# Half of the second block's weights split into seven operands during the first block and kept in DRAM

## The chip, the cores and the metric

The kernel runs on one core of one Trainium2 chip. The time is the device time of one execution in microseconds (us), as the median of several runs; lower is better. Every product is made in fp32r, with each operand split into a high part (a cast) and a low part (the rest), so that three matmuls stand for one.

## The reference

Three stages, one after another, on 8 batches of 576 tokens with 8 heads of 64 (512 columns). The second and third are cut here to their core:

```python
def _moe_ref(x, w_in, w_out):            # 512 -> 2048 -> 512
    h = x @ w_in
    g = np.where(h > 0.0, h, alpha * (np.exp(np.minimum(h, 0.0)) - 1.0))
    return (g @ w_out).astype(np.float32)

def _moe2_ref(x, w1, w2, w3, w_out):     # 512 -> 768 -> 512
    h = np.maximum(np.maximum(x @ w1, x @ w2), x @ w3)
    return (h @ w_out).astype(np.float32)
```

The first is an attention with landmarks: queries and keys averaged over groups of 18 tokens, three softmaxes, and six Newton steps for an inverse. The weights come as float64, so the kernel reads them as pairs of 32-bit words and makes float32 of them itself.

## The kernel before, in words

**First block** (attention and the first feed-forward). It runs batch by batch; a batch has 32 slots. In each slot `h_mm` makes a 128x288 piece of the hidden layer in 6 matmuls into a PSUM tile `ph` (two buffers), ACT makes two exponentials `eh` of it, DVE ends `eh`, `split` makes the two parts `gt` (cast on ACT, low part on POOL), and three slots later `x_mm` multiplies them by w_out in 12 matmuls. Attention of the next batch is laid into the slots by a table of slot numbers (`STEP_SLOTS`). The result goes to DRAM as `xs`. The order of PE and DVE in this block is the program's; `plan[t]` lists what else slot t issues.

**Weights of the second block.** `Narrowing` loads a piece of w1, w2, w3 (three pieces each, of 256 of the 768 columns) or of w_out2 (three pieces of 256 rows), makes float32 of it (`widen`, `narrow`) and stores it as `w2s` in DRAM. There are 12 pieces, two in each of batches 1 to 6.

**Second block.** 9 token blocks `nb` of 512 tokens, in each 3 pieces `p` of 256 hidden columns, in each the three weights `i`. One such product is `u_mm`: a 2x2 block product in Winograd's form with 7 products, 42 matmuls of 128x256. It needs seven token operands (`Operands`) and seven weight operands, each split in two. `quarters` combines the products (`s`, `v`, `u`, `t` on ACT, DVE and POOL), the maximum over `i` is taken on DVE, and `keep` makes three sums `s` of the four quarters `t` and stores all seven as `hs` in DRAM: already the operands of the output. The weight operands stay in SBUF for all token blocks. They are made by nine jobs `weights2(p, i)`: the raw piece is loaded from `w2s` (`raw2`), 4 differences `tt` on DVE, four or five casts `w` on ACT (L958), and low parts `w` (L960) on POOL and DVE in turn. The jobs begin in slot 2 of the last batch and go on, one step at each call of `background`, into the second block. Their places come free one by one: those of the first piece (`pools["w"]`) once attention is done, others where w_out of the first block was last read.

**Output.** For each token block two `o_mm` of 63 matmuls, `hs` against w_out2. `weights3` makes w_out2's seven operands (128x768, both parts) in the last token block: 4 differences, 7 casts (L1013), 7 low parts (L1015, on DVE and POOL in turn), into the seven tiles of the first piece's weights. `Middle` loads `hs` as seven `hf` and splits each into `ho` (cast L1092 on ACT; low part L1094 on DVE, the third operand's on POOL). The loads of the first three operands use the tag `s3` with three buffers, which `keep` uses too.

All transfers are issued by SP, in one order. Lines of the profile that the text speaks of: L101 and L103 `split`, L235 attention's products, L675 `h_mm`, L679, L680 and L685 `eh`, L707 `x_mm`, L791 `difference`, L824 and L826 the token operands, L861, L863 and L876 the sums of a product, L995 `u_mm`, L1104 `o_mm`.

Of the kernel before, what the change touches and what calls it, by code (L numbers as in the profile page):

```python
# [9 lines left out]
F32 = mybir.dt.float32  # L10
F32R = mybir.dt.float32r
# [8 lines left out]
def landmark_attention_mlp_maxout_kernel(  # L20
# [65 lines left out]
    NP = KF2 // 2  # L86
    w2s = tc.dram_tile([3 * NP + KF2 // 2, P, 1024], F32, name="w2s")
    hs = tc.dram_tile([NT // 512, P, NP, 7, 256], F32, name="hs")
# [671 lines left out]
    )  # L760

    class Narrowing:


        def __init__(self, it):
            self.it = it

        def load(self):
            t = att.tile([P, CH, DM], U32, tag="v", name="words2")
            self.words = t[:, :4].rearrange("p a (c w) -> p (a c) w", w=2)  # L770
            i, p = divmod(self.it, NP)
# [18 lines left out]
    def difference(out, a, b):  # L790
        nc.vector.tensor_tensor(out=out, in0=a, in1=b, op=ALU.subtract)  # L791

# [94 lines left out]
    N1 = 3 * len(OPS)  # L887

    def w_place(q):

# [31 lines left out]
    def raw2(n):  # L922
        p, i = divmod(n, 3)
        src = w2s[i * NP + p].rearrange("p (c f j) -> p c f j", c=KD, f=2)
# [8 lines left out]
    def weights2(p, i):  # L933

        n = 3 * p + i
        if n not in raws:
# [68 lines left out]

    def weights3():

        l = pools["l"]

        def put(nm, v, n):  # L1010
            t = l.tile([P, 2, NP, 256], F32R, tag=f"b{n}", name="wo2")
            hi, lo = wb[nm] = (t[:, 0], t[:, 1])
            nc.scalar.copy(hi, v)  # L1013
            eng = nc.gpsimd if n % 2 else nc.vector
            eng.tensor_tensor(out=lo, in0=v, in1=hi.bitcast(F32), op=ALU.subtract)  # L1015

        raw = [l.tile([P, NP, DM], F32, tag=tag, name="raw") for tag in ("xf", "b6")]
        for f in range(2):
            nc.sync.dma_start(
                out=raw[f],  # L1020
                in_=w2s[3 * NP :].rearrange("a p (f c) -> p f a c", f=2)[:, f],
            )
        s = l.tile([P, NP, 256], F32, tag="s3", name="s", bufs=3)
        b11, b12, b21, b22 = [t[:, :, e * 256 : (e + 1) * 256] for t in raw for e in range(2)]
        yield
        difference(s, b12, b11)
        put("T1", s, 0)
        yield
        difference(b12, b22, b12)
        put("T3", b12, 1)  # L1030
        yield
        put("B11", b11, 2)
        yield
        difference(s, b22, s)
        put("T2", s, 3)
        yield
        put("B21", b21, 4)
        yield
        put("B22", b22, 5)
        yield  # L1040
        difference(b11, b21, s)
        put("N4", b11, 6)
        yield


# [269 lines left out]
    for b in range(1, B):  # L1315
# [9 lines left out]
        for n in range(NCH):  # L1325
            at(t0 + NSL + (W_SLOTS if b > 1 else SECOND_W)[n], w_step, b, n, True)
    for it in range(3 * NP + KF2 // 2):
        nw = Narrowing(it)
        t0 = (1 + it // 2) * NSL + (15, 23)[it % 2]
        at(t0, nw.load)  # L1330
        run = nw.run()
        for n in range(4):
            at(t0 + 4 + n, next, run, None)
    manual = ExitStack()
    for t, sl in enumerate(seq):
# [8 lines left out]
        for fn in late:  # L1344
            if callable(fn):
                fn()
        if t >= LAG:
            x_mm(*seq[t - LAG])
        i = t - (B - 1) * NSL
        if i == 2:  # L1350
# [3 lines left out]
            tk = tokens(0)  # L1354
            jobs += [weights2(n // 3, n % 3) for n in range(9)]
        if i > KF and (i - KF) % FPN == FPN - 1:
            free += [f"wp{(i - KF) // FPN}{g}" for g in range(2)]
        if i > KF + LAG and (i - KF - LAG) % 2:
            passed.add((i - KF - LAG) // 2)
        if i > 2:  # L1360
# [8 lines left out]
    while tk.make():  # L1369
        pass  # L1370
    passed |= set(range(KF // 2))

    r_s.release()
# [6 lines left out]
        tc.tile_pool(name="ps_u", bufs=8, space=PSUM, reuse_waits="tile")  # L1380
    )


    for nb in range(NBL):
        nxt = tokens(nb + 1) if nb + 1 < NBL else None
        for p in range(NP):
# [27 lines left out]
    while len(ahead.raw) < len(OPS):  # L1414
        ahead.load()
    free += [(r_w, f"wo{m}") for m in range(5, KF // 2)]
# [59 lines left out]
```

## Time and profile before

| | before |
|---|---|
| time, median of 3 runs | 1374.45 us (1373.82 to 1375.12) |
| profiled execution | 1371.51 us |
| its span | 1369.7 us |
| PE busy | 1307.7 us (95%) |
| DVE busy | 842.6 us (62%) |
| ACT busy | 682.2 us (50%) |
| POOL busy | 678.8 us (50%) |
| DMA | 152.30 MB, 111 GB/s over the span |

The span is what the trace covers; the execution's time holds 1.8 us more. Busy time says which engine is full on average; the stages differ, so the prediction reads the trace stage by stage. The first block lasts until about 805 us, the second until 1225, the output until the end.

### The profile page before, as it was taken

Reading aid. Unit: us, or ns where it says so; the run is one execution under the profiler, and the core shown is the slowest. Engines: PE = TensorE matmul, PEld = TensorE weight load, DVE = VectorE, ACT = ScalarE, POOL = GpSimd, SP = SyncE. Lnnn points to the kernel's source line nnn. Section 1 sums busy time; section 2 is a strip of 40 time slices with the busy share of each in tenths; the row PEclk is TensorE's granted clock in tenths of the full one; section 3 lists DMA queues with packets and bytes.
Section 4 is the critical chain, followed back from the end, with each engine's and each line's share of the span. In section 5 each row is a group of like instructions: output and inputs, shape, how many; then the busy total and the mean of one; then the engine's idle time right before and its main releaser. Section 6 shows DMA issues by size and latency. Waiting matters only on the chain.

```text
span 1369.7 us, 28360 instructions
## 1 busy us (share of the span) xinstructions
PE 1307.7 (95%) x11144; PEld 1231.0 (90%) x11144; DVE 842.6 (62%) x1603; ACT 682.2 (50%) x1555; POOL 678.8 (50%) x671
## 2 busy tenths in 40 slices
PE   4588999999999999999999998999999999989998
PEld 2477899899998998998989998999999999989998
DVE  6885745436446455365453468776677667787673
ACT  4784556656656656566566643232133212345451
POOL 2781423424325334243355557666666666685543
PEclk8699999999999999999999999999999999999999
DMA  9635104204223042042132112221222122249882
GB/s 359 223 107 167 35 19 164 69 32 134 68 86 129 19 158 74 33 133 69 38 121 63 34 64 100 86 85 58 109 85 86 59 108 86 99 137 325 291 257 78
DMA packets 91590, 152.30 MB, mean 111 GB/s; under 512 B 5312, under 2 KB 49472, under 8 KB 91456
## 3 DMA queue, kind: packets, MB, share of 16 engines
q1 hardware_dynamic: 91456, 150.49, 32.0%
q8 instruction: 87, 1.43, 0.4%
q14 instruction: 47, 0.39, 0.1%
HBM read 99.35 MB, written 51.12 MB: 110 GB/s over the span
## 4 chain that ended last, share of the span: by engine, by line
PE 82%; DVE 6%; DMA 4%; ACT 3%; POOL 3%; issue 2%; SPq 0%; DVEq 0%; POOLq 0%; ACTq 0%
PE x L707 28%; PE p L995 24%; PE ph L675 14%; PE p L1104 10%; PE banks L235 6%; DMA words<-in_moe_w_out_dram 2%; DMA raw<-w2s 1%; POOL u L863 1%; DVE tt L791 1%; DMA kT<-in_k_dram 1%; ACT words L122 1%; DVE wf L128 0%; DMA hf<-hs 0%; ACT eh L679 0%; ACT gt L101 0%
## 5 line engine op out<-in xcount | busy, mean ns | idle before, releaser
L707 PE MATMUL x<-gt,wo 128*128 128x288 f32 x3072 | 468.0, 301 | 6.3 <-DVE gt L103 2.2
L707 PEld LDWEIGHTS x<-gt,wo 128*128 128x128 f32 x3072 | 422.0, 189 | 47.4 <-issue 22.3
L995 PE MATMUL p<-xo,w 128*128 128x256 f32 x3402 | 413.0, 284 | 7.2 <-ACT w L958 3.9
L995 PEld LDWEIGHTS p<-xo,w 128*128 128x128 f32 x3402 | 410.9, 191 | 9.4 <-ACT w L958 4.1
L103 POOL TENSOR_TENSOR gt<-eh,gt 128x288 fp32r<-128x288 f32 x243 | 198.0, 818 | 366.9 <-ACT gt L101 338.3
L675 PE MATMUL ph<-ah,wp 128*128 128x288 f32 x1024 | 249.6, 299 | 11.4 <-DVE eh L685 5.4
L685 DVE SCALAR_TENSOR_TENSOR eh<-eh,ph 128x288 f32<-128x288 f32 x256 | 114.2, 447 | 161.5 <-ACT eh L680 129.7
L863 POOL TENSOR_TENSOR u<-s,v 128x512 f32<-128x512 f32 x99 | 136.4, 1377 | 134.5 <-DVE v L861 134.5
L675 PEld LDWEIGHTS ph<-ah,wp 128*128 128x128 f32 x1024 | 180.3, 190 | 19.4 <-DVE eh L685 9.2
L679 ACT ACTIVATE eh<-ph 128x288 f32<-128x288 f32 x256 | 104.6, 410 | 125.8 <-PE ph L675 97.2
L101 ACT CAST gt<-eh 128x288 fp32r<-128x288 f32 x256 | 110.2, 431 | 112.0 <-DVE eh L685 111.6
L675 PE MATMUL ph<-al,wp 128*128 128x288 f32 x512 | 152.7, 298 | 2.1 <-POOL al L103 2.1
L852 ACT COPY s<-p 128x512 f32<-128x512 f32 x99 | 58.0, 586 | 173.5 <-PE p L995 135.1
L1104 PE MATMUL p<-wo,ho 128*128 128x256 f32 x1134 | 136.4, 283 | 3.8 <-ACT ho L1092 2.0
L1104 PEld LDWEIGHTS p<-wo,ho 128*128 128x128 f32 x1134 | 135.9, 191 | 4.2 <-ACT ho L1092 2.2
L680 ACT ACTIVATE eh<-eh 128x288 f32<-128x288 f32 x256 | 113.6, 445 | 5.3
L675 PEld LDWEIGHTS ph<-al,wp 128*128 128x128 f32 x512 | 97.3, 190 | 2.5 <-POOL al L103 2.5
L876 DVE TENSOR_TENSOR t<-p,u 128x512 f32<-128x512 f32 x81 | 55.7, 688 | 65.0 <-POOL u L863 62.7
L1002 DVE TENSOR_TENSOR t<-t 128x1024 f32<-128x1024 f32 x54 | 71.4, 1323 | 9.5 <-POOL t L866 3.8
L1094 DVE TENSOR_TENSOR ho<-hf,ho 128x768 fp32r<-128x768 f32 x54 | 65.4, 1237 | 17.4 <-ACT ho L1092 17.0
L1092 ACT CAST ho<-hf 128x768 fp32r<-128x768 f32 x63 | 51.3, 836 | 41.4 <-PE p L1104 22.5
L866 POOL TENSOR_TENSOR t<-u,s 128x256 f32<-128x256 f32 x81 | 67.7, 836 | 5.0
(167 smaller groups left out, 1387.5 us busy)
## 6 DMA issues: line engine op xcount, KB each, us to landing
hf<-hs SPq DMA_DIRECT2D x63, 384.0 KB, 5.6
hs<-t SPq DMA_DIRECT2D x27, 512.0 KB, 2.6
xs<-xo SPq DMA_DIRECT2D x36, 288.0 KB, 2.9
hs<-s SPq DMA_DIRECT2D x27, 384.0 KB, 2.9
qT<-in_q_dram SPq DMA_DIRECT2D x16, 576.0 KB, 6.3
kT<-in_k_dram SPq DMA_DIRECT2D x16, 576.0 KB, 7.4
words<-in_moe_w_dram SPq DMA_DIRECT2D x9, 1024.0 KB, 5.3
xf<-xs SPq DMA_DIRECT2D x9, 1024.0 KB, 5.0
```

Source lines behind the costliest of these rows:

```text
L101: nc.scalar.copy(hi, src)
L103: eng.tensor_tensor(out=lo, in0=src, in1=hi.bitcast(F32), op=ALU.subtract)
L235: ins = fn(*args, **kw)
L675: nc.tensor.matmul(ph[:, :HF], a, c, start=(g == 0 and j == 0), stop=(g == 1 and j == 2))
L679: nc.scalar.activation(e, ph[:, :HF], AF.Relu, scale=-1.0)
L680: nc.scalar.activation(e, e, AF.Exp, scale=-1.0)
L685: state["post"] = nc.vector.scalar_tensor_tensor(out=e, in0=e, scalar=1.0, in1=ph[:, :HF], op0=ALU.subtract, op1=ALU.max)
L707: nc.tensor.matmul(xacc[ec][:, :HF], a, gt[:, c], start=(first and j == 0), stop=(last and j == 2),)
L863: nc.gpsimd.tensor_tensor(out=u57, in0=s57, in1=v.unsqueeze(1).to_broadcast([P, 2, 256]), op=ALU.add)
L995: nc.tensor.matmul(dst, l, r, start=(c == 0 and j == 0), stop=(c == 1 and j == 2))
L1002: nc.vector.tensor_tensor(out=t, in0=t, in1=cur, op=ALU.max)
L1104: nc.tensor.matmul(dst, l, r, start=(c == 0 and n == 0), stop=(c == NP - 1 and n == 2))
```

## The change

Of the 12 pieces the three of w3 (`i == 2`) and the three of w_out2 are treated in a new way. `Narrowing` makes float32 of them as before, and in seven of the following slots (`behind`, slots 2 to 8 of the next batch) makes from them the seven operands in both parts, 4 differences `wt` on DVE, 7 casts `wq` on ACT, 7 low parts `wq` on POOL, and stores them as `wus` (w3) or `w3s` (w_out2). Their plain form isn't stored any more. In the second block `fetch_ready` loads w3's operands into the places where the jobs put them before (16 loads, 5.5 MB, where the raw pieces were 1.5 MB), and six jobs `weights2` are left. `fetch3` loads w_out2's operands, seven loads of 768 KB (5.5 MB, before 1.5 MB), after the first piece of the last token block; `weights3` is gone. All seven `hf` of the first output block are asked for after the second piece (before: five), with two more places for `ho`. The launch gets `dynamic_dma_scratch_size=1024`.

```diff
     class Narrowing:
-        def __init__(self, it):
-            self.it = it
+        def __init__(self, i, p):
+            self.i, self.p = i, p
...
-            for h, (_, f) in enumerate(halves):
-                nc.sync.dma_start(out=w2s[self.it][:, h * 512 : (h + 1) * 512], in_=f)
+            self.f = [f for _, f in halves]
+            if self.i < 2:
+                for h, f in enumerate(self.f):
+                    nc.sync.dma_start(
+                        out=w2s[self.i * NP + self.p][:, h * 512 : (h + 1) * 512], in_=f
+                    )
+
+        def put(self, nm, v):
+            k = [w for _, w in OPS].index(nm)
+            o = r_s.tile([P, 2, 256], F32R, tag="wq", name="wq", bufs=4)
+            hi, lo = [o[:, n] for n in range(2)]
...
+            split(v, hi, lo)
+            there = wus[:, self.p, k] if self.i < 3 else w3s[:, k, :, self.p]
+            nc.sync.dma_start(out=there, in_=o.bitcast(F32))
+
+        def parts(self):
...
+            t1, v1 = temp()
+            difference(v1, b12, b11)
+            self.put("B11", b11)
+            yield
+            t2, v2 = temp()
+            difference(v2, b22, v1)
+            self.put("T1", t1)
+            yield
...
+    def fetch_ready(q0, q1):
+        q = q0
+        while q < q1:
+            (u, k), (hi, lo, n) = divmod(q, 7), w_place(q)
+            n = min(n, q1 - q, 7 - k)
+            if u % 3 == 2:
+                for t, h in ((hi, 0), (lo, 1)):
+                    nc.sync.dma_start(out=t[:, :n].bitcast(F32), in_=wus[:, u // 3, k : k + n, h])
...
-    def weights3():
...
+    def fetch3():
+        for k in range(len(OPS)):
+            t = pools["l"].tile([P, 2, NP, 256], F32R, tag=f"b{k}", name="wo2")
+            nc.sync.dma_start(out=t.bitcast(F32), in_=w3s[:, k])
+            wb[OPS[k][1]] = [t[:, h] for h in range(2)]
...
-    for it in range(3 * NP + KF2 // 2):
-        nw = Narrowing(it)
-        t0 = (1 + it // 2) * NSL + (15, 23)[it % 2]
-        at(t0, nw.load)
-        run = nw.run()
-        for n in range(4):
-            at(t0 + 4 + n, next, run, None)
+    plain = [(i, p) for p in range(NP) for i in range(2)]
+    split7 = [(2, p) for p in range(NP)] + [(3, p) for p in range(NP)]
+    behind = [[] for _ in range(len(seq))]
+    for it in range(2 * NP):
+        for n, (nw, t0) in enumerate(((Narrowing(*plain[it]), 15), (Narrowing(*split7[it]), 23))):
+            t0 += (1 + it) * NSL
+            at(t0, nw.load)
+            run = nw.run()
+            for m in range(3):
+                at(t0 + 4 + m, next, run, None)
+            if n:
+                parts = nw.parts()
+                for m in range(7):
+                    behind[t0 + 11 + m].append(parts)
...
-            jobs += [weights2(n // 3, n % 3) for n in range(9)]
+            fetch_ready(0, N1)
+            jobs += [weights2(n // 2, n % 2) for n in range(2 * NP)]
...
+            fetch_ready(N1 + 4 * m, N1 + 4 * m + 4)
...
             if nxt is None and p == 0:
-                jobs.append(weights3())
+                fetch3()
...
-                for _ in range(5):
+                for _ in OPS:
                     ahead.load()
...
+                free += [(pools["r"], f"e{n}") for n in range(2)]
```

The order of PE's instructions is the same in both kernels. On the others instructions move, at three places above all. (Line numbers in the rows are those of each kernel; the changed one has them two higher in the first block; there `difference` is L765, the sums of a product are L916, L925 and L931, `raw` is loaded in L995, `xf` in L1037. A number behind a name tells tiles of that name apart.)

**ACT in the first slots of a middle batch.** `xo` ends a half of the batch before, `e` is attention's softmax. Before:

```order
L733 COPY xo<-x_2660 128x288
L101 CAST gt<-eh 128x288
L679 ACTIVATE eh<-ph 128x288
L680 ACTIVATE eh<-eh 128x288
L101 CAST gt<-eh 128x288
L679 ACTIVATE eh<-ph 128x288
L680 ACTIVATE eh<-eh 128x288
L337 COPY e<-banks 128x288 x2
L101 CAST gt<-eh 128x288
L679 ACTIVATE eh<-ph 128x288
L680 ACTIVATE eh<-eh 128x288
L337 COPY e<-banks 128x288 x2
```

With the change:

```order
L735 COPY xo<-x_2662 128x288
L103 CAST gt<-eh 128x288
L103 CAST wq<-wt 128x256
L103 CAST wq<-wf_2948 128x256 x2
L681 ACTIVATE eh<-ph 128x288
L682 ACTIVATE eh<-eh 128x288
L681 ACTIVATE eh<-ph 128x288
L103 CAST gt<-eh 128x288
L103 CAST wq<-wt 128x256
L682 ACTIVATE eh<-eh 128x288
L339 COPY e<-banks 128x288 x2
L103 CAST gt<-eh 128x288
```

Between the exponentials now stand the casts `wq`, three in one slot and one in each of those that follow.

**SP at the start of the last batch**, where the second block's first loads are issued (`xf` tokens, `raw` plain pieces). Before:

```order
L788 DMA w2s<-wf_8977 128x512
L788 DMA w2s<-wf_8980 128x512
L969 DMA xf<-xs 128x4x512
L927 DMA raw<-w2s 128x4x128
L927 DMA raw<-w2s 128x2x128 x2
L927 DMA raw<-w2s 128x4x128
L927 DMA raw<-w2s 128x2x128 x2
```

With the change:

```order
L809 DMA w3s<-wq 128x2x256
L1037 DMA xf<-xs 128x4x512
L952 DMA w_9431<-wus 128x4x256
L952 DMA w_9432<-wus 128x4x256
L952 DMA w_9433<-wus 128x3x256 x2
L995 DMA raw<-w2s 128x4x128
L995 DMA raw<-w2s 128x2x128 x2
L995 DMA raw<-w2s 128x4x128
L995 DMA raw<-w2s 128x2x128
```

Four loads of ready operands (`w<-wus`) stand ahead of the raw pieces.

**DVE in the last token block**, from the second piece's first product on (`v`, `t` sums of a product, L1002 or L1070 the maximum, `raw` w_out2). Before:

```order
L861 TENSOR_TENSOR v<-p_15118,s_15135 128x256
L870 TENSOR_TENSOR t<-p_15142,s_15135 128x256
L791 TENSOR_TENSOR raw<-raw 128x3x256
L1015 TENSOR_TENSOR wo_15198<-raw,wo_15198 128x768
L1015 TENSOR_TENSOR wo_15126<-s,wo_15126 128x768
L876 TENSOR_TENSOR t<-p_15154,u_15139 128x512
L791 TENSOR_TENSOR s<-raw,s 128x768
L861 TENSOR_TENSOR v<-p_15191,s_15207 128x256
L870 TENSOR_TENSOR t<-p_15214,s_15207 128x256
L791 TENSOR_TENSOR raw<-raw,s 128x3x256
L1015 TENSOR_TENSOR wo_15239<-raw,wo_15239 128x768
L876 TENSOR_TENSOR t<-p_15225,u_15211 128x512
```

With the change, the same products:

```order
L916 TENSOR_TENSOR v<-p_15294,s_15307 128x256
L925 TENSOR_TENSOR t<-p_15314,s_15307 128x256
L931 TENSOR_TENSOR t<-p_15322,u_15311 128x512
L916 TENSOR_TENSOR v<-p_15352,s_15365 128x256
L925 TENSOR_TENSOR t<-p_15372,s_15365 128x256
L931 TENSOR_TENSOR t<-p_15380,u_15369 128x512
L1070 TENSOR_TENSOR t<-t 128x1024
```

The differences and low parts of w_out2 are gone from between the products' sums.

## Rows read from the trace of the kernel before

**Rows 1.** The windows by stage: stretch, length, busy of each engine, granted clock, DMA share, GB/s.

```profile
205.00:297.20 92.20, 92.20 (x828) 84.39 (x827) 48.16 (x119) 55.87 (x139) 34.59 (x41) 1.00 0.26 87
805.10:880.20 75.10, 68.05 (x543) 67.43 (x544) 59.72 (x88) 24.85 (x52) 49.07 (x44) 0.95 0.26 88
880.20:1176.00 295.80, 295.80 (x2456) 294.64 (x2455) 201.53 (x304) 78.78 (x159) 189.01 (x176) 1.00 0.22 85
1225.00:1250.30 25.30, 21.46 (x158) 21.05 (x157) 17.46 (x23) 11.60 (x18) 15.30 (x12) 0.87 0.79 260
1250.30:1365.30 115.00, 114.96 (x980) 114.75 (x979) 74.04 (x89) 53.09 (x80) 52.98 (x40) 1.00 0.71 236
```

**Rows 2.** PE's waits between 805 and 881 us: releaser, total us, times, longest.

```profile
PE p L995 <- ACT w L958: 3.9, 1, 3.9
PE p L995 <- ACT xo L824: 1.7, 1, 1.7
PE p L995 <- POOL w L960: 1.5, 1, 1.5
```

**Rows 3.** The window after PE's first long wait in the output.

```profile
1232.00:1236.00 4.00, 3.45 (x16) 3.45 (x17) 2.78 (x4) 0.83 (x1) 1.46 (x3) 0.50 0.07 17
```

**Rows 4.** PE's waits between 1200 and 1260 us.

```profile
PE p L1104 <- ACT ho L1092: 2.0, 1, 2.0
PE p L1104 <- POOL ho L1094: 1.8, 1, 1.8
```

**Rows 5.** PE's timeline at the start of the output: start, duration, and idle before.

```profile
1224.99 2.27 PE L1104 MATMUL p<-wo,ho 128*128 128x256 f32 x18
1229.30 1.44 PE L1104 MATMUL p<-wo,ho 128*128 128x256 f32 x10 [2.03 <-ACT ho L1092]
```

**Rows 6.** SP's timeline, the loads of `hf` behind the last stores.

```profile
1224.74 11.57 SPq L1079 DMA_DIRECT2D hf<-hs  x6
```

**Rows 7.** ACT's timeline, the third operand's high part.

```profile
1228.41 0.83 ACT L1092 CAST ho<-hf 128x768 fp32r<-128x768 f32 x1 [2.54 <-DMA hf<-hs]
```

**Rows 8.** POOL's timeline: an `u` of the last piece, and the third operand's low part.

```profile
1220.18 1.30 POOL L863 TENSOR_TENSOR u<-s,v 128x512 f32<-128x512 f32 x1 [3.29 <-DVE v L861]
1230.68 1.81 POOL L1094 TENSOR_TENSOR ho<-hf,ho 128x768 fp32r<-128x768 f32 x1
```

**Rows 9.** DVE's timeline in the last token block.

```profile
1202.96 2.61 DVE L1015 TENSOR_TENSOR wo<-s,wo 128x768 fp32r<-128x768 f32 x1
1222.74 0.95 DVE L1094 TENSOR_TENSOR ho<-hf,ho 128x768 fp32r<-128x768 f32 x1
```

**Rows 10.** The window in which w_out2's operands are made.

```profile
1200.00:1212.00 12.00, 12.00 (x102) 12.00 (x101) 11.05 (x11) 5.55 (x10) 12.00 (x7) 1.00 0.19 76
```

**Rows 11.** Groups by line and form, 700 to 880 us: count, busy, mean ns, idle before.

```profile
L958 ACT CAST w<-raw 128x256 fp32r<-128x256 f32 x9 | 3.6, 404 | 3.0 <-DMA raw<-w2s 2.1 <-PE x L707 0.9
L960 POOL TENSOR_TENSOR w<-raw,w 128x256 fp32r<-128x256 f32 x9 | 8.5, 946 | 0.0
L791 DVE TENSOR_TENSOR tt<-raw 128x256 f32<-128x256 f32 x18 | 11.4, 651 | 2.1 <-DMA raw<-w2s 2.1
```

**Rows 12.** DVE's timeline in the handover: one operation at two durations.

```profile
840.37 1.40 DVE L791 TENSOR_TENSOR tt<-raw,tt 128x256 f32<-128x256 f32 x1
850.15 0.41 DVE L791 TENSOR_TENSOR tt<-raw,tt 128x256 f32<-128x256 f32 x1
```

**Rows 13.** DVE's timeline in a middle batch.

```profile
464.24 0.45 DVE L685 SCALAR_TENSOR_TENSOR eh<-eh,ph 128x288 f32<-128x288 f32 x1 [2.19 <-ACT eh L680]
```

**Rows 14.** PE's timeline there: the next slot's first product.

```profile
465.58 0.29 PE L675 MATMUL ph<-ah,wp 128*128 128x288 f32 x1
```

**Rows 15.** PE's timeline: the last read of `w_in_sb`.

```profile
723.74 1.09 PE L235 MATMUL banks<-w_in_sb,mt 64*32 64x512 f32 x16
```

**Rows 16.** ACT's timeline: the first cast of a weight piece.

```profile
730.25 0.61 ACT L958 CAST w<-raw 128x512 fp32r<-128x512 f32 x1
```

**Rows 17.** The page's DMA issues: count, KB each, us to landing.

```profile
hf<-hs SPq DMA_DIRECT2D x63, 384.0 KB, 5.6
```

More of the change, by code (lines that the diff above doesn't have):

```diff
@@ L86, in landmark_attention_mlp_maxout_kernel @@
     NP = KF2 // 2
-    w2s = tc.dram_tile([3 * NP + KF2 // 2, P, 1024], F32, name="w2s")
+    w2s = tc.dram_tile([2 * NP, P, 1024], F32, name="w2s")
+    wus = tc.dram_tile([P, NP, 7, 2, 256], F32, name="wus")
+    w3s = tc.dram_tile([P, 7, 2, NP, 256], F32, name="w3s")
     hs = tc.dram_tile([NT // 512, P, NP, 7, 256], F32, name="hs")
@@ L760, in landmark_attention_mlp_maxout_kernel, with difference @@
     )
+    def difference(out, a, b):
+        nc.vector.tensor_tensor(out=out, in0=a, in1=b, op=ALU.subtract)
     class Narrowing:
-        def __init__(self, it):
-            self.it = it
+        def __init__(self, i, p):
+            self.i, self.p = i, p
         def load(self):
@@ L786, in run, with temp @@
                 yield
-            for h, (_, f) in enumerate(halves):
-                nc.sync.dma_start(out=w2s[self.it][:, h * 512 : (h + 1) * 512], in_=f)
-    def difference(out, a, b):
-        nc.vector.tensor_tensor(out=out, in0=a, in1=b, op=ALU.subtract)
+            self.f = [f for _, f in halves]
[8 more added lines that the diff above has]
+            hi, lo = [o[:, n] for n in range(2)]
+            if self.i < 3 and nm[0] == "B":
+                hi, lo = [t.rearrange("p (c j) -> p c j", c=2) for t in (hi, lo)]
+            split(v, hi, lo)
+            there = wus[:, self.p, k] if self.i < 3 else w3s[:, k, :, self.p]
+            nc.sync.dma_start(out=there, in_=o.bitcast(F32))
+        def parts(self):
+            if self.i < 3:
+                b11, b12, b21, b22 = [
+                    f.rearrange("p (c h j) -> p c h j", c=2, h=2)[:, :, e]
+                    for f in self.f
+                    for e in range(2)
+                ]
+            else:
+                b11, b12, b21, b22 = [f[:, e * 256 : (e + 1) * 256] for f in self.f for e in range(2)]
+            def temp():
+                t = r_s.tile([P, 256], F32, tag="wt", name="wt", bufs=4)
+                return t, (t.rearrange("p (c j) -> p c j", c=2) if self.i < 3 else t)
+            t1, v1 = temp()
[6 more added lines that the diff above has]
+            yield
+            t3, v3 = temp()
+            difference(v3, b22, b12)
+            self.put("B22", b22)
+            yield
+            t4, v4 = temp()
+            difference(v4, b21, v2)
+            self.put("B21", b21)
+            yield
+            self.put("T2", t2)
+            yield
+            self.put("T3", t3)
+            yield
+            self.put("N4", t4)
+            yield
     class Operands:
@@ L887, in landmark_attention_mlp_maxout_kernel @@
     N1 = 3 * len(OPS)
+    def fetch_ready(q0, q1):
[6 more added lines that the diff above has]
+                    nc.sync.dma_start(out=t[:, :n].bitcast(F32), in_=wus[:, u // 3, k : k + n, h])
+                for m in range(n):
+                    wb[u // 3, 2, OPS[k + m][1]] = (hi[:, m], lo[:, m])
+            q += n
     def w_place(q):
@@ L922, in raw2 @@
     def raw2(n):
-        p, i = divmod(n, 3)
+        p, i = divmod(n, 2)
         src = w2s[i * NP + p].rearrange("p (c f j) -> p c f j", c=KD, f=2)
@@ L933, in weights2 @@
     def weights2(p, i):
-        n = 3 * p + i
+        n = 2 * p + i
         if n not in raws:
@@ L1003, in u_mm @@
         return t
-    def weights3():
[L1008 to L1043, printed above, removed]
+    def fetch3():
[3 more added lines that the diff above has]
+            wb[OPS[k][1]] = [t[:, h] for h in range(2)]
     KEPT = (4, 1, 0, 5, 2, 6, 3)
@@ L1346, in landmark_attention_mlp_maxout_kernel @@
                 fn()
+        for parts in behind[t]:
+            next(parts, None)
         if t >= LAG:
@@ L1358, in landmark_attention_mlp_maxout_kernel @@
         if i > KF + LAG and (i - KF - LAG) % 2:
-            passed.add((i - KF - LAG) // 2)
+            m = (i - KF - LAG) // 2
+            passed.add(m)
+            fetch_ready(N1 + 4 * m, N1 + 4 * m + 4)
         if i > 2:
@@ L1371, in landmark_attention_mlp_maxout_kernel @@
     passed |= set(range(KF // 2))
+    fetch_ready(N1 + 2 * KF - 8, N1 + 2 * KF)
     r_s.release()
@@ L1381, in landmark_attention_mlp_maxout_kernel @@
     )
+    fetch_ready(N1 + 2 * KF, 3 * N1)
     for nb in range(NBL):
@@ L1408, in landmark_attention_mlp_maxout_kernel @@
                 ahead = Middle(0)
-                for _ in range(5):
+                for _ in OPS:
                     ahead.load()
                 free = [(r_w, f"wo{m}") for m in range(5)]
+                free += [(pools["r"], f"e{n}") for n in range(2)]
         tk = nxt
-    while len(ahead.raw) < len(OPS):
-        ahead.load()
     free += [(r_w, f"wo{m}") for m in range(5, KF // 2)]
```

4 lines of the change are left out of this document (2 added, 2 removed).

## The prediction, made before the changed kernel ran

> **What bounds the kernel now.** I read the windows by stage first, then what PE waits for in the two stages where it isn't full, then the timelines around those waits. The windows show that TensorE sets the time nearly everywhere: in a middle batch of the first block it is busy for 92.20 of 92.20 us, in the steady part of the second block for 295.80 of 295.80, in the output for 114.96 of 115.00, at a granted clock of 1.00 [rows 1]. What can be won lies in the two rows that are left, the handover into the second block (805.1 to 880.2 us, clock 0.95) and the start of the output (1225.0 to 1250.3, clock 0.87) [rows 1].
>
> Their loss is worked out against the steady stage of the same products. Second block: 295.80/2456 = 0.1204 us a matmul [rows 1]; the handover has 543 of them, 65.4 us at that pace, and takes 75.1. **9.7 us are lost**; 3.9 + 1.7 + 1.5 = 7.1 us of that are PE waiting, for a weight's high part from ACT, an `xo` and a weight's low part from POOL [rows 2], and the remaining 2.6 lie in the clock. Output: 114.96/980 = 0.1173 us [rows 1]; 158 of them are 18.5 us, and the stretch takes 25.3. **6.8 us are lost**; 2.0 + 1.8 = 3.8 us are PE waiting for `ho`, ACT's and then POOL's [rows 4], and the other 3.0 again the clock: after these waits the granted clock is 0.50, the lower of the two levels (1.2 GHz) [rows 3]. So ending the waits should give their clock back as well.
>
> Why they occur. In the handover DVE is busy for 59.72 of 75.10 us [rows 1] with the token operands, the sums of the products and the last four weight jobs; the 3.9 us wait is for an ACT cast which itself waits for DVE's differences. In the last token block making w_out2's operands fills DVE for 11.05 and POOL for 12.00 of 12 us [rows 10], a single low part taking 2.61 [rows 9]. The backlog is still there in the last piece: POOL waits 3.29 us for DVE's `v` [rows 8]. The store of `keep` is late by it, and behind that store SP issues the load of the third operand at 1224.74 [rows 6]; ACT casts it at 1228.41 [rows 7], POOL makes its low part from 1230.68, in 1.81 us [rows 8]. PE had come to it at 1224.99 + 2.27 = 1227.3 [rows 5].
>
> **The change, part by part.**
>
> *Second block, weights of w3.* Three of the nine `weights2` jobs go; of the four that DVE still had to do in the handover, one is left. What takes their place are loads only, and the handover moves no more than 88 GB/s at a DMA share of 0.26 [rows 1], so they have room; the loads for the second and third piece are let go by the last matmuls of the first block and are wanted some 25 and 40 us later (five and eight products of 42 × 0.1204 = 5.06 us, [rows 1]). I take the whole 9.7 us as gone, and put 0.5 back for what isn't the weights' fault: the 1.7 us for `xo` [rows 2] need not vanish, so bounds 0 to 1.7, nearer to 0 because that operand was late behind the same DVE queue.
>
> *Last token block, w_out2.* Seven casts, seven low parts and four differences become seven loads of 768 KB. 5.5 MB at the 260 GB/s of the output's start [rows 1] are 21 us, over the 30 us that the second and third pieces take before the output (six products); all seven are issued ahead of the third operand's load, and none waits for an engine that is behind. With the backlog gone, the third operand's load is set by the buffer that it takes over: it must wait until DVE has made the low part of the first operand. The last piece's first group ends on PE two products before the output, 1224.99 − 2 × 5.06 = 1214.9 [rows 1, 5]; its `v`, `u` (1.30, [rows 8]), `t` and two `ho` of 0.95 [rows 9] put the load at about 1219 instead of 1224.74. It lands 5.6 us later (median of such loads, [rows 17]), at 1224.6; cast 0.83, low part 1.81 [rows 7, 8]: 1225.4 and 1227.3. PE wants the high part at 1227.3 and the low part some ten matmuls later, at 1228.5 [rows 5]. That is in time by 1 to 2 us, so the whole 6.8 us is taken as gone, with a margin thin enough to be a rival.
>
> *First block, batches 2 to 7.* Each gets seven parts: 7 ACT casts of 128x256 (0.40 us, [rows 11]: 2.8 us a batch), 4 DVE differences (0.65: 2.6 us), 7 POOL low parts (0.95: 6.6 us) and 7 stores of 256 KB on SP, two stores of the plain piece less for half of them. The engines have the time: 55.87, 48.16 and 34.59 us are used of 92.20 [rows 1]. The stores add at most 1.8 MB in 92.2 us, 19 GB/s to 87 [rows 1]. What can hurt is the place: the casts stand in slots 2 to 8, where ACT also does the exponentials of attention, and `eh` on DVE sets when PE may reuse `ph`'s two buffers. The tightest place that I found has DVE ending `eh` at 464.24 + 0.45 = 464.69 [rows 13], and PE starting the product that needs it at 465.58 [rows 14]: 0.9 us of slack, and there ACT would now carry a cast or two (0.4 to 0.8). Elsewhere it is wider. Cost: nothing in most batches, a few tenths in some; 0.5 us over six batches. Bounds 0 and 7 (every batch loses three casts, 1.2 us). SP's loads of q, k, v and words stand behind the new stores, which wait for POOL's low parts; those loads are issued half a batch ahead, and this cover hides it.
>
> *Start of the last batch.* Loads of 512, 512, 384 and 384 KB now stand on SP ahead of the raw pieces, and the first must wait until PE has read `w_in_sb` for the last time, 723.74 + 1.09 = 724.8 [rows 15]. 1.8 MB at 260 GB/s [rows 1] take 6.9 us: 731.7; the first raw piece (512 KB, 2.0 us) is there at about 734, while ACT cast from it at 730.25 [rows 16]. ACT waits some 3.5 us with `eh` casts queued behind; `ph`'s second buffer covers at most a slot, 92.2/32 = 2.9 us [rows 1]. I put 1.0 us; bounds 0 (the transfers run at full rate, or the cast is reached later) and 5 (the whole wait).
>
> **Sum.** The profiled execution took 1371.5 us (span 1369.7 and 1.8 around it). 1371.5 − 9.7 + 0.5 − 6.8 + 0.5 + 1.0 = 1357.0. That execution lies 2.9 us below the median of the three timed runs, 1374.45; the forecast for the median is **1360 us**. A difference of less than 0.2% (2.7 us) can't be told from none.
>
> **A rule against it.** One DVE difference of two SBUF operands, 128x256, takes 0.41 us when undisturbed and 1.40 us in the same stretch beside POOL [rows 12]; so POOL's work delays DVE. The Trainium skill, "SBUF — State Buffer", section "SBUF: two separate sides", says that such a DVE operation and a GpSimd one share a port pair as an exclusive lock: who comes second waits for the whole instruction. The rows agree in direction (1.0 us added is about one POOL instruction). The first block gets 7 POOL instructions and 4 such differences a batch; if each difference met one and `eh` stood behind it, that is rival 2.
>
> **The rivals.**
>
> 1. *Only the handover pays.* The third operand is late again: its load stands behind seven transfers of 768 KB and SP's other stores, and a landing 2 us later eats the margin. As one late operand also costs the clock, take the whole 6.8 back: 1367. For it: 1 to 2 us of margin against landing times up to 5.6 us [rows 17]. Against: the load itself is released 5 us sooner. Chance 0.14.
> 2. *Slower: the first block pays.* In slots 2 to 8 of batches 2 to 7 the seven casts (0.40 each) and four differences held up by a POOL instruction (0.95 each, [rows 11]) all stand ahead of an `eh`. 2.8 + 3.8 − 0.9 of slack = 5.7 us a batch, 34 in six: 1394. It decides from (16.5 − 1.5 + 2.7)/6 = 3.0 us a batch on, that is if over half of this is unhidden. Against it: ACT is free for 39% and DVE for 48% of the stage [rows 1], and `ph` has two buffers. Chance 0.06.
> 3. *The waits change their name.* 8 MB more are loaded through the same queue, and in this program each transfer waits for the one eight places before it; if the loads of w3's pieces or w_out2 come as late as their making did, the gain is given back: 1374. Against it: room for 25 us and more, DMA share 0.26 [rows 1]. Chance 0.05.
>
> **How the numbers follow.** The forecast has 0.75, the rivals 0.14, 0.06 and 0.05. The forecast's own bounds: −1.5 (no price anywhere) to +8 (7 and 5 aren't met together) give 1358.5 to 1368, and 3 us of run-to-run difference between median and profiled execution widen that below, to 1355. The range 1355 to 1368 takes in rival 1. Faster by over 0.2% means under 1371.7: the forecast and rival 1, less their upper tails, 0.87; within 0.2%: rival 3 and a little of the tails, 0.06; slower 0.07.
>
> **What would show it.** In the changed kernel's windows, PE busy for the whole handover at clock 1.00 and its 543 matmuls in 65 to 67 us; the output's first 158 in 18.5 to 20. SP issues the third operand's load near 1219 less what was won before it. PE's waits in the first block stay under 1 us a batch, and the one at the start of the last batch under 3. Wrong would be: a PE wait for `eh` in every middle batch (rival 2), for a `w` or `wo` landing by DMA (rival 3), or for the third `ho` (rival 1).

## The result, and the profile after

The changed kernel takes **1359.28 us** (median of 4 runs, 1357.23 to 1359.97), the kernel before beside it 1374.78 us (4 runs, 1373.82 to 1376.08): a ratio of 0.9884 with a 95% interval of 0.9867 to 0.9901, or 15.5 us. The profiled execution took 1358.94 us with a span of 1357.2.

The windows by stage, cut at the same matmuls as before: from PE's 1000th matmul to the start of the second block, its first 543 matmuls, the stretch up to the last token block, the output's first 158 matmuls, and its last 834, those behind the first 300 (the expectations below call this stretch the last 843; columns as in [rows 1]):

```profile
163.07:806.44 643.37, 640.80 (x5613) 590.56 (x5612) 338.06 (x814) 399.56 (x1012) 282.40 (x336) 1.00 0.29 96
806.44:871.93 65.49, 65.44 (x543) 65.25 (x544) 46.26 (x68) 18.74 (x39) 42.10 (x38) 1.00 0.32 109
871.90:1167.60 295.70, 295.70 (x2455) 294.55 (x2454) 200.57 (x304) 78.69 (x159) 188.83 (x176) 1.00 0.22 85
1216.63:1237.15 20.52, 18.82 (x160) 18.62 (x160) 16.64 (x20) 10.57 (x16) 11.98 (x10) 1.00 0.80 263
1254.00:1352.85 98.85, 98.85 (x835) 98.85 (x834) 59.33 (x72) 40.38 (x63) 43.64 (x34) 1.00 0.64 209
```

The handover and the output's start of the kernel before, cut at these matmuls too, a little off the rounded windows of [rows 1]:

```profile
805.06:880.28 75.22, 68.15 (x543) 67.54 (x544) 59.81 (x89) 24.85 (x52) 49.07 (x44) 0.95 0.26 88
1224.98:1250.57 25.59, 21.75 (x160) 21.34 (x159) 17.48 (x23) 11.87 (x18) 15.59 (x13) 0.87 0.79 261
```

Against these, the handover takes 65.5 us instead of 75.2 at a clock of 1.00 instead of 0.95, DVE being busy for 46.3 us of it instead of 59.8; the steady stage is the same ([rows 1]); the output's start takes 20.5 us instead of 25.6, again at 1.00. PE has a single wait left in each of the two stages, which answer to [rows 2] and [rows 4]:

```profile
PE p L1063 <- DVE xo L737: 1.0, 1, 1.0
```

```profile
PE p L1138 <- ACT ho L1126: 1.7, 1, 1.7
```

The chain behind the third operand of the output, as in [rows 5 to 8]: SP's loads, SP's wait before the first of them, ACT's cast, POOL's low part, and PE.

```profile
1211.61 11.64 SPq L1113 DMA_DIRECT2D hf<-hs  x6
```

```profile
SPq L1113 <- DVE ho L1128: 1.9, 1, 1.9
```

```profile
1215.28 0.83 ACT L1126 CAST ho<-hf 128x768 fp32r<-128x768 f32 x1 [5.19 <-DMA hf<-hs]
```

```profile
1216.19 1.85 POOL L1128 TENSOR_TENSOR ho<-hf,ho 128x768 fp32r<-128x768 f32 x1 [1.23 <-ACT ho L1126]
```

```profile
1216.68 17.06 PE L1138 MATMUL p<-wo,ho 128*128 128x256 f32 x144
1235.43 4.78 PE L1138 MATMUL p<-wo,ho 128*128 128x256 f32 x38 [1.70 <-ACT ho L1126]
```

The third operand's load is the first of SP's six. It is issued 5.1 us ahead of the output's first matmul (before: 0.25), the cast is over at 1216.1 and the low part at 1218.0, while PE comes to that operand at 1216.68 + 2.27 = 1218.95. PE now runs through 144 matmuls, one and a seventh token block, and then waits 1.70 us for the third operand of the *second* token block. In the 12 us that answer to [rows 10] DVE and POOL are half idle, and the transfers have taken their place (DMA share 0.85):

```profile
1191.70:1203.70 12.00, 12.00 (x102) 12.00 (x101) 6.76 (x10) 3.91 (x7) 5.95 (x6) 1.00 0.85 324
```

The profiled executions differ by 12.5 us: +1.3 that is there before the thousandth matmul, where the new work hasn't begun (161.8 and 163.1 us), +0.1 in the first block, −9.7 in the handover, −5.1 at the output's start and +0.2 behind it, +1.1 in the last 834 matmuls, −0.4 after the last.

### The profile page after: what moved, and what is told of

Its sections match the earlier page's. It is cut to its first block, busy times and chain, and to the rows that moved or that the text cites. A ratio compares the mean times of both kernels' runs of the same rounds, so it can differ in the third digit from the quotient of the medians.

```text
span 1357.2 us, 28503 instructions
## 1 busy us (share of the span) xinstructions
PE 1302.8 (96%) x11144; PEld 1228.0 (90%) x11144; DVE 832.5 (61%) x1601; ACT 678.1 (50%) x1576; POOL 690.0 (51%) x702
## 4 chain that ended last, share of the span: by engine, by line
PE 84%; DMA 5%; ACT 3%; DVE 3%; issue 2%; POOL 2%; SPq 0%; DVEq 0%; ACTq 0%; POOLq 0%
PE p L1063 28%; PE x L709 27%; PE ph L677 13%; PE p L1138 9%; PE banks L237 6%; DMA words<-in_moe_w_out_dram 2%; DMA hf<-hs 1%; DMA hs<-t 1%; ACT words L124 1%; DMA kT<-in_k_dram 1%; DMA words<-in_moe_w_dram 0%; ACT gt L103 0%; ACT wf L121 0%; DVE wp L650 0%; POOL wf L133 0%
## 5 line engine op out<-in xcount | busy, mean ns | idle before, releaser
L918 POOL TENSOR_TENSOR u<-s,v 128x512 f32<-128x512 f32 x99 | 132.1, 1334 | 148.4 <-DVE v L916 148.4
L931 DVE TENSOR_TENSOR t<-p,u 128x512 f32<-128x512 f32 x81 | 55.7, 688 | 72.7 <-POOL u L918 70.0
L1128 DVE TENSOR_TENSOR ho<-hf,ho 128x768 fp32r<-128x768 f32 x54 | 71.8, 1361 | 13.2 <-ACT ho L1126 12.3
L1070 DVE TENSOR_TENSOR t<-t 128x1024 f32<-128x1024 f32 x54 | 69.4, 1285 | 6.5 <-POOL t L921 0.4
L921 POOL TENSOR_TENSOR t<-u,s 128x256 f32<-128x256 f32 x81 | 67.1, 829 | 5.5
L916 DVE TENSOR_TENSOR v<-p,s 128x256 f32<-128x256 f32 x99 | 41.5, 419 | 46.0 <-ACT s L914 46.0
```

The source lines that it names most:

```text
L918: nc.gpsimd.tensor_tensor(out=u57, in0=s57, in1=v.unsqueeze(1).to_broadcast([P, 2, 256]), op=ALU.add)
```

## The experiments

All numbers of this table come from windows cut at the same matmuls: the first block from the 1000th matmul on, the handover's 543, the output's first 158 and last 834. The last two columns are the timed median beside that of the kernel before on the same chip, and the ratio.

| kernel | first block | handover | output's start | output's rest | medians | ratio (95%) |
|---|---|---|---|---|---|---|
| before | 643.26 | 75.22 | 25.59 | 97.74 | | |
| changed | 643.37 | 65.49 | 20.52 | 98.85 | 1359.28 / 1374.78 | 0.9884 (0.9867 to 0.9901) |
| 1 w3 only | 643.73 | 67.56 | 26.90 | 97.74 | 1367.33 / 1373.4 | 0.9953 (0.9937 to 0.9970) |
| 2 w_out2 only | 645.65 | 75.70 | 21.08 | 97.74 | 1373.0 / 1373.4 | 0.9996 (0.9982 to 1.0010) |
| 3 made, unused | 646.37 | 75.00 | 27.63 | 97.75 | 1379.69 / 1373.4 | 1.0041 (1.0028 to 1.0053) |
| 4 small edits only | 643.32 | 74.59 | 29.45 | 98.85 | 1379.15 / 1373.4 | 1.0043 (1.0026 to 1.0060) |
| 5 without the small edits | 643.74 | 67.25 | 19.45 | 98.84 | 1361.04 / 1375.0 | 0.9900 (0.9881 to 0.9918) |
| 6 loads, no places | 642.75 | 68.31 | 23.22 | 97.74 | 1365.78 / 1375.0 | 0.9933 (0.9916 to 0.9950) |
| 7 no differences of w3 | 642.78 | 75.89 | 27.46 | 98.85 | 1374.14 / 1375.0 | 0.9997 (0.9984 to 1.0010) |
| 8 parts doubled | 648.12 | 65.49 | 21.01 | 97.74 | 1365.06 / 1375.0 | 0.9928 (0.9911 to 0.9945) |
| 9 steps without work | 642.56 | 70.79 | 27.40 | 98.85 | 1369.74 / 1375.63 | 0.9953 (0.9936 to 0.9970) |
| 10 changed, again | 646.02 | 65.46 | 21.49 | 97.73 | 1360.73 / 1375.63 | 0.9886 (0.9864 to 0.9908) |
| 11 as 5, no last steps | 644.68 | 67.11 | 19.47 | 98.84 | 1358.81 / 1375.63 | 0.9881 (0.9866 to 0.9895) |
| 12 changed, no last steps | 645.72 | 65.47 | 21.69 | 97.74 | 1360.66 / 1375.63 | 0.9891 (0.9876 to 0.9906) |

**1 and 2: each half alone.** From the changed kernel, run 1 stores w_out2's pieces plain and takes `weights3` back, and with it the early loads and the two places of the output's start, the "small edits" of runs 4 to 6; run 2 stores w3's pieces plain and takes the nine jobs back.

```diff
-            if n:
+            if n and it < NP:          # run 2: if n and it >= NP
                 parts = nw.parts()
...
-                fetch3()               # run 1
+                jobs.append(weights3())
...
-            fetch_ready(0, N1)         # run 2
-            jobs += [weights2(n // 2, n % 2) for n in range(2 * NP)]
+            jobs += [weights2(n // 3, n % 3) for n in range(3 * NP)]
```

> Only w3's pieces are made into operands in the first block; w_out2 is made in the last token block as before. My theory (two separate gains): the first 543 matmuls of the second block take 65 to 67 us instead of 75.1, the output's first 158 stay at 24 to 26 us with PE waits for ho of about 3.8; about 9.7 us faster than before, 1365. Rival (the gains hang together, relief in the handover also brings the output's start): output's start at 20 us, about 1360. Rival (the handover needs both halves' relief): handover still above 71, 1371 or more.

> Only w_out2's pieces are made into operands in the first block; the nine weight jobs of the second block stay. My theory: the handover stays at 74 to 76 us, the output's first 158 matmuls take 20 us as in the changed kernel; about 5 us faster than before, 1370. Rival (the output's start is gained by w3's half or by nothing here): 1374 to 1375.

Run 1 had 7.7 of the handover's 9.7 us and nothing at the output, run 2 had 4.5 of the output's 5.1 and nothing in the handover, so each gain comes from the half from which it was forecast. But both were slower than expected (1367.3 for 1365, 1373.0 for 1370), and the halves don't add up: 6.1 and 0.4 us, against 15.5 together. The windows of run 2 show where its gain of 4.5 us at the output went, first block, handover, output's start:

```profile
164.34:809.99 645.65, 641.93 (x5614) 590.65 (x5613) 332.22 (x799) 396.26 (x992) 269.24 (x317) 1.00 0.26 84
809.99:885.69 75.70, 68.16 (x543) 67.50 (x543) 59.73 (x89) 24.84 (x52) 49.09 (x44) 0.95 0.26 88
1230.38:1251.46 21.08, 19.06 (x162) 18.86 (x161) 16.31 (x20) 10.32 (x15) 12.01 (x10) 0.99 0.79 268
```

The first block is 2.4 us longer, and the waits say why:

```profile
PE ph L677 <- DVE eh L687: 1.5, 3, 0.6
PE x L709 <- POOL gt L105: 0.7, 1, 0.7
```

One of the three waits for `eh`, of 0.6 us, lies at 786 us, and the kernel before has it too. The other two and the one for `gt` lie between 740 and 746 us, in the first slots of the last batch, and the 2.4 us arise there. In these slots w_out2's last parts now meet nine weight jobs that have started: ACT's cast waits for two of DVE's differences, the first of which takes 1.51 us while POOL makes low parts, and the exponentials stand behind the cast.

```profile
740.10 0.62 ACT L1026 CAST w<-tt 128x512 fp32r<-128x512 f32 x1 [1.86 <-DVE tt L765]
```

In the changed kernel there are six jobs, and the raw pieces come later. Another 1.3 us go behind the output's start (17.95 us for the next 142 matmuls, 16.66 before). Run 1's handover has a wait that the changed kernel hasn't, 2.1 us for an `xo` from ACT; run 5 has it too and shows where it comes from.

**3: made and stored, but not used.** The second block of the kernel before behind the first block of the change, with all plain pieces stored too.

```diff
-            if self.i < 2:
+            if True:
                 for h, f in enumerate(self.f):
```

> All operands are made and stored in the first block as in the change (and the plain pieces stored too), but the second block makes them again as before and never reads them. My theory: the first block's extra work costs 0 to 0.5 us in the stage from batch 2 on; 1374.5 to 1376 in all, handover and output as before (75 and 25 us). Rival (the 1.4 us by which the changed kernel reaches the second block later is the price of the new work): 1.4 us and more appear within batches 2 to 7, 1376 to 1378.

It is 6.3 us slower than the kernel before. Of the 3.1 us in the first block 2.4 are the same meeting in the last batch as in run 2 (ACT's cast waits 1.86 us there as well); the batches up to there have 0.7, a little over the theory's 0 to 0.5. The theory had overlooked the last batch with all nine jobs. The profile has 2.0 us more at the output's start and 1.9 in the second block behind the handover, 1.3 of these one wait for an `xo`; both were expected as before, and no run shows where they come from.

**4 to 6: the small edits.** Run 4 is the kernel before with seven `hf` asked for early, the two places and the launch argument. Run 5 is the changed kernel with five and no places, run 6 with seven and no places. The launch argument was not changed by itself.

```diff
-                for _ in OPS:          # run 5
+                for _ in range(5):
                     ahead.load()
...
-                free += [(pools["r"], f"e{n}") for n in range(2)]     # runs 5 and 6
```

> The kernel before with only the small edits: all seven hf asked for after the second piece, two more places for ho, the launch argument. My theory (the gain at the output's start comes from the work taken off DVE and POOL): no change, 1374 to 1375.5, output's first 158 matmuls at 24 to 26 us. Rival (it comes from the earlier loads and the places): 20 us there, 1370.

> The changed kernel with the small edits at the output's start taken back: five hf asked for after the second piece, the last two after the third, no places e0 and e1. From the run with these edits alone, in which the output's first 158 matmuls took 29.5 us instead of 25.6 and the 843 last matmuls 98.85 instead of 97.74, theory A (they cost, and the gain there is the relief of DVE and POOL alone): first 158 in at most 21 us, the last 843 in 97.7; 1356 to 1358.5. Theory B (without weights3 they are what lets the operands come in time): first 158 in 23 us or more, 1361 or more.

> The changed kernel with only the two places e0 and e1 taken back; all seven hf are still asked for after the second piece. If the places set the pace of the output's last 843 matmuls (98.85 us in the two kernels that have them together with seven loads, 97.74 in the others but one), it is 97.74 here; if the early loads set it, 98.85. The time follows: 1358 in the first case, 1359.3 in the second.

Run 4 excludes the rival: these edits don't bring the gain at the output's start. The theory's "no change" missed as well, by 5.8 us: with DVE still behind, the stretch takes 29.45 us, where the kernels without them (before, runs 1, 3, 7, 9) have 25.6 to 27.6:

```profile
PE p L1104 <- ACT ho L1092: 5.2, 2, 4.3
PE p L1104 <- DVE ho L1094: 1.8, 2, 1.2
```

In the changed kernel they cost about 1 to 2 us there: without them the stretch is 19.45 (run 5), with them 20.52 and 21.49 (run 10), with the loads but without the places 23.22 (run 6). The relief alone is thus 25.6 − 19.5 = 6.1 us, as theory A had it. But runs 5 and 6 took 1361.04 and 1365.78 us in all, where at most 1358.5 and 1359.3 were expected: what the edits give back is in the handover, where none of them acts: 67.25 and 68.31 us without the places, 65.5 with them. The windows of run 5, handover and output's start:

```profile
808.00:875.25 67.25, 65.41 (x543) 65.21 (x544) 47.38 (x69) 18.66 (x39) 41.72 (x38) 1.00 0.31 106
1219.96:1239.41 19.45, 18.82 (x160) 18.63 (x160) 15.79 (x19) 10.48 (x16) 10.85 (x9) 1.00 0.83 281
```

SP's timeline there, first of the changed kernel, then of run 5 (the loads of the third piece's ready operands):

```profile
807.49 4.27 SPq L952 DMA_DIRECT2D w<-wus  x6
```

```profile
811.52 3.16 SPq L952 DMA_DIRECT2D w<-wus  x6
```

They go out 1.1 us after the second block's start in the one, 3.5 us in the other. In the program the first of them waits for PE and POOL with the places, and without them for the store of the first block's last `xo` as well: the two places shift the tiles of that pool, and without them the operands lie where that `xo` lay. SP's waits in the stage's first 9 us agree, first of the changed kernel, then of run 5:

```profile
SPq L952 <- DMA xs<-xo: 0.6, 2, 0.4
```

```profile
SPq L952 <- DMA xs<-xo: 2.8, 2, 2.5
```

Behind these loads SP issues the last raw piece, and DVE begins the differences of the last job 0.8 us later in its stage than in the changed kernel. Later DVE comes to the next token operands, the first of the same four operations in each:

```profile
849.18 0.68 DVE L881 TENSOR_TENSOR xo<-xf,xo 128x512 fp32r<-128x512 f32 x1
```

```profile
851.48 1.78 DVE L881 TENSOR_TENSOR xo<-xf,xo 128x512 fp32r<-128x512 f32 x1
```

And POOL to its two:

```profile
849.25 3.49 POOL L881 TENSOR_TENSOR xo<-xf,xo 128x512 fp32r<-128x512 f32 x2 [1.24 <-ACT xo L879]
```

```profile
850.83 3.58 POOL L881 TENSOR_TENSOR xo<-xf,xo 128x512 fp32r<-128x512 f32 x2 [0.53 <-ACT xo L879]
```

In the changed kernel DVE begins 0.07 us ahead of POOL and takes 0.68 us; in run 5 it begins 0.65 us after POOL and takes 1.78 us, the next two take 1.78 and 1.66 (changed kernel: 1.38 and 1.11), and PE waits 1.75 us for an `xo`. The pattern repeats: this first operation takes 0.68 or 0.69 us in the changed kernel's two profiles and 1.77 to 1.79 in runs 1, 5, 6 and 11, the kernels without the places. That the store is what delays the loads, and this delay what turns the order of DVE and POOL, is read from the program and the traces; no run changed it alone. Whether early loads or places set the output's rest (98.85 or 97.74 us) is answered by neither: run 5 has 98.84, run 6 97.74, and run 10 is the changed kernel with 97.73.

**7 and 9: what in w3's jobs makes the handover late.** Run 7 leaves out their 12 DVE differences, run 9 all their work, while their steps stay.

```diff
+        if i == 2:
+            tt = raw                   # run 7
+        else:
             difference(tt[:, 0], raw[:, 3], raw[:, 0])
...
+        if i == 2:                     # run 9: the same number of steps
...
+                    wb[p, i, nm] = wb[p, 0, nm]
...
+                yield
+            return
```

> The kernel before without DVE's 12 differences for w3 (the operands T1, T2, T3 and N4 of w3 are cast from the plain pieces, so those products are others); loads, casts and low parts stay. My theory (DVE's queue is what makes the handover's operands late): PE's 3.9 us wait for the cast of w vanishes with its clock loss, the first 543 matmuls of the second block take 66 to 70 us instead of 75.2; 1365 to 1370. Rival (ACT's and POOL's part or the transfers make them late): still 73 us or more, 1373 or more.

> The kernel before in which w3's three jobs keep their places and steps among the nine but do nothing: no loads, differences, casts or low parts; the products of w3 read w1's operands (so they are others). Theory A (the work of w3's jobs, on whichever engine, makes the handover's operands late): first 543 matmuls of the second block in 65.5 to 68 us, as in the kernels with ready operands; 1364 to 1368. Theory B (it is the number of steps: with three jobs fewer the later jobs of w1 and w2 come earlier, before the second block begins, and that is the gain): they stay above 70 us, 1369 or more.

Run 7 contradicts the theory: the 3.9 us wait for the cast is gone, and the handover is no shorter (75.9 us); PE waits for other work instead:

```profile
PE p L1000 <- ACT xo L824: 2.3, 1, 2.3
PE p L1000 <- POOL w L965: 1.8, 1, 1.8
PE p L1000 <- DVE xo L826: 1.8, 1, 1.8
PE p L1000 <- DVE w L965: 1.5, 2, 1.2
```

DVE is busy for nearly as long as before (59.1 us in 83 instructions, 59.8 in 89): the ones that are left take longer. Run 9 takes out all the work and gets 4.4 of the 9.7 us, which leaves it at theory B's figure:

```profile
802.96:873.75 70.79, 67.12 (x542) 66.70 (x543) 54.91 (x79) 20.65 (x43) 45.18 (x42) 0.98 0.22 79
```

No wait for a weight is left there; PE waits twice for an `xo`:

```profile
PE p L1013 <- DVE xo L826: 1.8, 1, 1.8
PE p L1013 <- ACT xo L824: 1.7, 1, 1.7
```

The other part is the order. The steps of the jobs are laid one by one into the slots; with three jobs fewer, those of w1 and w2 come earlier. Of DVE's differences for the jobs 16 fall into the handover before, 8 in run 9 and 4 in the kernels with the jobs gone. Those without the places (runs 1, 5, 6, 11) have 67.1 to 68.3 us. So of the 9.7, taken in this order: 4.4 for the work, 2.5 to 3.7 for the steps (from 70.8 to these), 1.6 to 2.8 for the tiles that the places shift (from these to 65.5).

**8: the parts doubled.**

```diff
             split(v, hi, lo)
+            split(v, hi, lo)
             there = wus[:, self.p, k] if self.i < 3 else w3s[:, k, :, self.p]
```

> The changed kernel with the cast and the low part of each of the 42 operands in the first block made twice (the differences and stores once). My theory (the first block has room at these places): 0 to 3 us more in all, 1359 to 1362. Rival (the room is just used up): PE waits for eh in each of the six batches, 6 us or more, 1365 and above.

4 to 6 us slower than the changed kernel's two medians, between the two theories in the first block and at the rival's edge in all. The first block is 648.12 us, 4.8 longer than the first profile of the changed kernel and 2.1 than the second, with PE waiting for `gt` and `eh`:

```profile
PE x L709 <- POOL gt L105: 1.5, 1, 1.5
PE ph L677 <- DVE eh L687: 1.4, 4, 0.4
```

So there is room for the new work once, and little more: not every batch pays, as the rival had it, but against the mean of the six profiles with the work done once, 644.4 us (below), the doubling costs 3.7.

**10 to 12: the changed kernel again, and two attempts to better it.** Runs 11 and 12 make no step of a weight job in the first block's last three slots, run 11 from run 5, run 12 from the changed kernel.

```diff
         x_mm(*seq[t - LAG])
         tk.make()
-        background()
     vector.close()
```

> The changed kernel once more, unaltered. If the pace of the last 843 matmuls (98.85 or 97.74 us) and the wait for xo in the handover (0 in the first profile; 1.7 to 2.1 in three kernels of the same order there) belong to the execution and not to the kernel, one of them differs from its first profile; if they belong to the kernel, both repeat: 98.85 and no wait. 1357 to 1361 in either case.

> The run without the small edits, and in addition no step of a weight job in the last three slots of the first block, so that DVE copies xo there at once. My theory: PE's 1.0 us wait for DVE's copy of xo at the second block's start goes, the first 158 of the output stay at 19.5 us; 1 us less than without this, 1358.5 to 1360.5. Rival (the steps come later and make a weight or xo late in the handover): a wait of 1 us or more there takes its place.

> The changed kernel with only that edit: no step of a weight job in the last three slots of the first block. My theory: the 1.0 us wait goes, 1357.5 to 1359.5. Rival: as in the run before, a wait in the handover in its place, 1359.5 and above.

Run 10, first block, handover, output's start and rest:

```profile
162.97:808.99 646.02, 642.09 (x5616) 590.91 (x5614) 337.99 (x813) 399.33 (x1013) 282.43 (x336) 1.00 0.29 95
808.99:874.45 65.46, 65.04 (x540) 64.87 (x541) 46.50 (x69) 18.66 (x39) 42.00 (x38) 1.00 0.32 110
1219.15:1240.64 21.49, 19.58 (x162) 19.38 (x162) 17.06 (x21) 10.96 (x17) 12.78 (x10) 0.97 0.79 262
1258.08:1355.81 97.73, 97.73 (x835) 97.73 (x835) 60.02 (x73) 40.39 (x63) 43.49 (x34) 1.00 0.64 212
```

The handover repeats to 0.03 us. The output's rest doesn't, and the first block is 2.7 us longer than in the first profile, 1.1 of it one wait for `eh`. Both attempts missed: the wait of 1.0 us for DVE's copy of `xo` is still there in each; what stands ahead of the copy had been issued in earlier slots. Their medians, 1358.81 and 1360.66, can't be told from the changed kernel's 1359.28 and 1360.73. The runs point to a kernel with five early loads and the shift of the two places kept, 65.5 and 19.5 us, some 1 to 2 us better; it wasn't tried.

## Why the prediction was right

**The time.** 1360 us were forecast in a range of 1355 to 1368; it was 1359.28. The profiled execution was forecast at 1357.0 and took 1358.94; 1.3 of the difference arose before the change acts, 1.1 in the pace of the output's rest. That the sum fits is partly luck: against the first profile its terms are off by −0.5 (handover), +1.7 (output's start) and −1.4 us (first block), which nearly cancel.

**The handover**: forecast −9.7 and +0.5, measured −9.7. The size was right, and the clock came back with the waits (0.95 to 1.00), as forecast; the reason was partly another. "I take the whole 9.7 us as gone" rested on DVE's work; run 9 gives 4.4 us to the work of w3's jobs, and the rest falls to the other jobs' coming earlier (2.5 to 3.7) and to the two places. Four jobs in DVE's order had become one, as the text said, but only two of the three that went were w3's. And the 1.7 us for `xo`, which were to go "because that operand was late behind the same DVE queue", don't go with that queue: they stay without the two places (1.6 to 2.1 us in runs 1, 5, 6 and 11). That step of the forecast was wrong, and an edit priced at nothing made up for it.

**The output's start**: forecast −6.8, measured −5.1 (−4.1 in run 10), so 20.5 and 21.5 us where 18.5 to 20 were to show it. The mechanism is shown: with DVE and POOL relieved, the third operand's load goes out 5.1 us ahead of the output (forecast: 6.0), released by a low part that DVE makes, as forecast, and its parts are there 2.8 and some 2 us before PE wants them (forecast: 1 to 2). The step that was off is "the whole 6.8 us is taken as gone": relief alone gives 6.1 (run 5), and the early loads, which weren't priced, take 1 to 2 back, as the wait for the second token block's third operand.

**The first block**: forecast 0.5 + 1.0, measured +0.1 and +2.8 in two profiles of the same kernel; over the six profiles with this first block (the changed one twice, runs 5, 6, 11, 12) 642.75 to 646.02, mean 644.4, against 643.3 in the kernel before and run 4. So about 1.1, no more than what two executions of one kernel differ by. Compared matmul by matmul with the kernel before, it lies in the middle batches, which were to cost 0.5: up to the middle of the last batch (765 us in the kernel before) the six are behind by 0.15, 2.81, 0.53, −0.43, 1.41 and 1.78 us, 1.0 in the mean. The start of the last batch, which was to cost 1.0, costs nothing in any of them. The step that failed there is "ACT waits some 3.5 us": ACT comes to its first cast of a plain piece later than before (730.25, [rows 16]), behind the casts `wq` and the exponentials, and goes on without a gap.

```profile
737.02 0.91 ACT L1026 CAST w<-raw 128x512 fp32r<-128x512 f32 x2
```

The 1.0 us for `xo` at the block's end is nearly made up by a wait for `eh` in the kernel before, at 781 us, which the changed kernel hasn't and which costs 0.9 us with what follows it:

```profile
PE ph L675 <- DVE eh L685: 0.6, 1, 0.6
```

The bound of 7 us was far; run 8 with twice the work has 4.8.

**The rivals.** Rival 1, only the handover pays, is run 1 and not the change. Rival 2, the first block pays, needed 3.0 us a batch; the whole block has 0.1 to 2.8, and even doubled 0.8 a batch. The rule on the shared port pair of the Trainium skill, "SBUF — State Buffer", section "SBUF: two separate sides", names its mechanism, and the rows of the changed kernel and of run 5 agree with it (a DVE operation on two SBUF operands at 0.68 us when it begins ahead of POOL and at 1.78 when it begins after). What it cost shows in the handover and, in runs 2 and 3, at the start of the last batch, not in every middle batch. Rival 3 didn't occur: none of PE's waits names a load of the new operands.

## What to carry to other kernels

Work moved to an earlier stage pays if that stage has idle slots at the place where it is put, and it must be counted together with what else starts there: the half in run 2 gained 4.5 us at the output's start and lost 2.4 of them in the first block and 1.3 behind that start; the two halves together lost 0.1 to 2.8 in the first block. A wait shows who came last, not what would have to go: here the wait named one engine's cast, and taking its cause away only moved the wait; the steps of the schedule and the order of the jobs behind them had to go too. And edits that look like bookkeeping (two more tiles in a pool) move the others, and with them what a load has to wait for.

## What the runs showed of the hardware that was not expected

- The output's last 834 matmuls take either 97.74 us (before and runs 1, 2, 3, 6, 8, 10, 12) or 98.85 (the changed kernel's first profile and runs 4, 5, 7, 9, 11), nothing in between, with PE busy throughout and a granted clock of 1.00 in both. It is a pace and no single event: all along the stretch 63 matmuls take 7.39 us in the one and 7.47 to 7.48 in the other. The same kernel shows both (first profile and run 10), so it belongs to the execution; what sets it stays open.
- The thousandth matmul comes between 160.4 and 164.7 us in these profiles. So a single profiled execution says little about 2 us of the total, and the windows between the same matmuls say more.
